# Engine orders, PSUM banks and transfer holds written out as lists, in a gated linear attention followed by a gated feed-forward layer

## The chip, the cores and the metric

The kernel runs on one core of one Trainium2 chip. The metric is the time of one execution in device microseconds (us); lower is better. Five engines work side by side, each with an order of its own: PE (TensorE, the matmuls), ACT (ScalarE), DVE (VectorE), POOL (GpSimd) and SP (SyncE, which here only issues transfers). PE writes only to PSUM, which has eight banks; ACT and DVE read PSUM. DMA engines carry data between HBM and SBUF and, as "DMA transposes", from SBUF to SBUF.

## What is computed

The reference is an attention with a decaying state, then a feed-forward layer (B=4 batches, H=8 heads, S=768 tokens, D=48; model width 384, inner width 1536):

```python
f = 1.0 / (1.0 + np.exp(-f_logit))
for t in range(S):
    state = f[:, :, t, :, None] * state + np.einsum('bhd,bhe->bhde', k[:, :, t], v[:, :, t])
    y[:, :, t] = np.einsum('bhd,bhde->bhe', q[:, :, t], state)
...
gate = np.maximum(x @ w_gate, 0.0)
val = x @ w_val
return (gate * val @ w_out).astype(np.float32)
```

x is y with the heads side by side: 3072 tokens of width 384.

## The kernel before

The sequence is cut into six steps (c = 0 to 5) of 128 tokens. In a step each of the four batches (b) goes through the same attention. ACT turns f_logit into minus the log of the gate (Exp at L631, Ln at L633). PE sums it over the tokens of the step with a triangular matrix ("cum", L640) and over the whole step with a column of ones (L643). ACT takes two exponentials of the sums (L650, L652). POOL multiplies k and q with them; the results are the "hats" (L662, L665). The hats have to be turned so that the head dimension lies on partitions (tile `qkT`): for steps 1 and 2 with PE transposes and a DVE copy (L676, L681), for steps 3 to 5 with a DMA transpose issued by SP (L684). PE forms the scores (L706), DVE masks them into `ptm` (L711), POOL casts v to bf16 (`vpad`, L697). PE adds the part that comes from the old state and the part of the step itself: for steps 0 to 2 in a form that comes out already turned (L733) and that ACT copies to `xT` (L750), for steps 3 to 5 in the natural form (L739, L743), which ACT copies to `xn` (L756) and SP turns by DMA. PE forms k^T v (L767), and DVE and POOL update the state (L480, L482).

Step 0 has a form of its own (`attention_four`, L485, and `attention_back`, L605). Its f, k and q are loaded by `load_four` (L375) with four consecutive tokens of one head in each run of 768 bytes, so that four tokens lie on a partition; all four batches are worked on together, with four cumulative sums for every output (L515, L520), transposes at L555, scores at L574 and masks at L581. `attention_back` turns the k hats back (L613, L618). All other loads (`load`, L393) carry two batches of a step with runs of 192 bytes, 384 KB in each.

The feed-forward part of a step works on all 512 tokens of the four batches. For each of the 12 blocks j of 128 inner units PE forms gate and value (L796, three matmuls each), ACT takes the ReLU of the gate (L802), DVE multiplies (L806) into `gT`. In steps 0 and 1 the first blocks are done for batches 0, 1 and 2, 3 apart, so that the layer can begin when two batches are ready. Then, for each batch, 12 matmuls of 384 columns with `wo` (L819) form the output; ACT copies it (L829), SP stores it.

The weights are read by POOL's transfers, which convert to bf16 (`load_w`, L408): three slices each of `wg`, `wv` and `wo`, four blocks j in each.

The order of the work is set by a list scheduler (`Plan.schedule`, L90): every operation has an engine, an estimated duration and a priority, and the scheduler places one after another at the earliest moment that it estimates, giving PSUM banks from limits by group ("f": 4, "s": 4 and so on, L294). `follows` keeps loads in the order of the step; `flight = 3` makes a load wait until the third load ahead of it has landed (L845); `floor` and "@" in `first` (L233) hold back the first loads. Ahead of the first operations PE multiplies zeros 512 columns wide (L869 to L892), as many as fit in the gaps of the estimate. The engines run their lists in order; between engines there are semaphores (`needs`, L171).

Of the kernel before, what the change touches and what calls it, by code (L numbers as in the profile page):

```python
# [9 lines left out]


class Op:


    __slots__ = ("eng", "emit", "reads", "writes", "occ", "lat", "prio", "opens", "deps",
                 "idx", "start", "end", "pos", "inc", "sem", "val", "snap", "n_left", "users", "ready",
                 "after", "follows", "flow", "goal", "floor")

    def __init__(self, eng, emit, reads, writes, occ, lat, prio, opens=(), after=(), follows=()):
        self.eng, self.emit, self.reads, self.writes = eng, emit, reads, writes  # L20
        self.occ, self.lat, self.prio, self.opens = occ, lat, prio, list(opens)
        self.after, self.follows = list(after), list(follows)
        self.users = []
        self.inc = False
        self.sem = None
        self.val = 0
        self.start = None
        self.flow = None
        self.floor = 0.0


class Bank:


    def __init__(self, group):
        self.group = group
        self.ap = None
        self.ops = []
        self.slot = None


class Plan:


    ENGINES = ("PE", "ACT", "DVE", "POOL", "SP")

    def __init__(self, limits):
        self.ops = []
        self.limits = limits
        self.free0 = {e: 0.0 for e in self.ENGINES}  # L50

    def add(self, eng, emit, reads=(), writes=(), occ=0.5, lat=0.2, prio=0, opens=(), after=(), follows=()):
        op = Op(eng, emit, list(reads), list(writes), occ, lat, prio, opens, after, follows)
        op.idx = len(self.ops)
        self.ops.append(op)
        return op

    def link(self):
        writers, readers = {}, {}
        for op in self.ops:  # L60
            deps = {}
            for d in op.after:
                deps[d] = "raw"
            for d in op.follows:
                deps[d] = "order"
# [4 lines left out]
            for t in op.writes:  # L70
                for r in readers.get(t, ()):
                    if r is not op and deps.get(r, "order") == "order":
                        deps[r] = "war"
                for w in writers.get(t, ()):
                    if w is not op and deps.get(w, "order") == "order":
                        deps[w] = "war"
# [3 lines left out]
            for t in op.writes:  # L80
                if t in op.reads or isinstance(t, Bank):
                    writers.setdefault(t, []).append(op)
                else:
                    writers[t] = [op]
                    readers[t] = []
# [4 lines left out]
    def schedule(self, banks):  # L90
        self.link()
        for op in self.ops:
            op.n_left = len(op.deps)
            op.ready = op.floor
            for d in op.deps:
                d.users.append(op)
        free = dict(self.free0)
        waiting = {e: [] for e in self.ENGINES}
        order = {e: [] for e in self.ENGINES}
        for op in self.ops:  # L100
            if op.n_left == 0:
                waiting[op.eng].append(op)
        slots = [{"ap": ap, "tile": None, "at": at} for ap, at in banks]
        used = {}
        left = len(self.ops)
        flow_free = 0.0

        def banks_for(op):
            n, group = len(op.opens), op.opens[0].group
            if used.get(group, 0) + n > self.limits[group]:  # L110
                return None
            idle = [s for s in slots if s["tile"] is None or all(o.start is not None for o in s["tile"].ops)]
            idle.sort(key=lambda s: s["at"])
            return idle[:n] if len(idle) >= n else None

        while left:
            pick = None
            for e in self.ENGINES:
                for op in waiting[e]:
                    at = max(free[e], op.ready)  # L120
                    slot = ()
                    if op.opens:
                        slot = banks_for(op)
                        if slot is None:
                            continue
                        at = max(at, slot[-1]["at"])
                    key = (at, op.prio, op.idx)
                    if pick is None or key < pick[0]:
                        pick = (key, op, slot)
            if pick is None:  # L130
                raise RuntimeError("no op can be scheduled: " + repr(
                    [(e, len(waiting[e])) for e in self.ENGINES]))
            (at, _, _), op, slot = pick
            e = op.eng
            waiting[e].remove(op)
            for tile, s in zip(op.opens, slot):
                if s["tile"] is not None:
                    for o in s["tile"].ops:
                        op.deps[o] = "war"
# [831 lines left out]
```

## Time and profile before

| what | value |
|---|---|
| median of 3 runs (lowest, highest) | 210.68 us (207.79, 211.08) |
| span of the profiled execution | 208.5 us (a time of its own is not listed beside it) |
| mean granted TensorE clock | 0.967 |
| busy: PE, ACT, DVE, POOL | 191.4, 110.5, 105.1, 79.6 us |
| first matmul of the feed-forward layer | 29.28 us |
| end of the last matmul | 205.66 us |
| bytes read from and written to HBM | 25.95 MB, 4.72 MB |

The span is the time from the first to the last instruction. Busy is the sum of the durations on an engine; a matmul's duration holds its way through the array, so that a row of matmuls on PE counts as busy also where they follow one another less closely than they could. A line of a group reads: line of the code, engine, operation, output and inputs by the program's names, shape, count, busy time, mean duration in ns. "idle before" is the time in which the engine waited ahead of such instructions, and what ended the wait. The chain of waits starts at the last instruction and goes back, at each step, to what released it. In a table by stretches of time, the columns are the time from and to, its length, each engine's busy time with the count of instructions, the granted clock of TensorE, the share of time in which the 16 DMA engines were occupied (over 1 where transfers overlap on them), and GB/s.

### The profile page before, as it was taken

What the parts mean: (1) busy time and instruction counts of PE and PEld (TensorE: products, weight loads), DVE (VectorE), ACT (ScalarE), POOL (GpSimd) and SP (SyncE); (2) the same over time, 40 slices, a digit from 0 to 9 for tenths busy, and PEclk for the clock granted to TensorE, in tenths of its full rate; (3) what the DMA queues carried; (4) which work ended last, traced back from release to release, by engine and by line L of the source; (5) the groups of instructions that cost most, each with busy time, mean ns of one, the idle gap of its engine ahead of it and who ended that gap; (6) DMA issues with size and microseconds to landing.
All of it is one profiled execution on the core that took longest, in us unless ns stands there. A gap on an engine that the chain in (4) does not pass through costs nothing.

```text
span 208.5 us, 4328 instructions
## 1 busy us (share of the span) xinstructions
PE 191.4 (92%) x1724; PEld 110.0 (53%) x1743; DVE 105.1 (50%) x183; ACT 110.5 (53%) x239; POOL 79.6 (38%) x112
## 2 busy tenths in 40 slices
PE   7835779999999799999999999997999999999994
PEld 2414449645677576455555555553545554445562
DVE  7008376643818878657376444634545333323210
ACT  2741224583488678876747756555434334443411
POOL 8806910027196875967553654413500000000000
PEclk9995758999999999999999999999999999999999
DMA  4997899999599999999889999988961111111112
GB/s 130 263 209 152 118 199 190 188 232 211 120 223 237 227 187 197 168 207 204 172 192 138 196 222 160 218 161 145 206 154 36 46 38 41 38 38 38 38 51 103
DMA packets 115076, 31.74 MB, mean 152 GB/s; under 512 B 105072, under 2 KB 115056, under 8 KB 115056
## 3 DMA queue, kind: packets, MB, share of 16 engines
q1 hardware_dynamic: 111072, 27.93, 65.7%
q0 software_dynamic: 3984, 3.54, 10.9%
q8 instruction: 14, 0.23, 0.4%
q14 instruction: 6, 0.05, 0.1%
HBM read 25.95 MB, written 4.72 MB: 147 GB/s over the span
## 4 chain that ended last, share of the span: by engine, by line
PE 84%; DMA 5%; SPq 3%; DVE 2%; ACT 2%; issue 2%; DVEq 0%
PE ps L796 45%; PE ps L819 22%; DMA q_in<-in_q_dram 4%; SPq L385 3%; PE ps L706 3%; PE ps L733 2%; PE ps L767 2%; PE ps L676 2%; PE ps L640 2%; DMA qkT<-hats 1%; PE ps L555 1%; PE ps L880 1%; PE ps L743 1%; PE ps L739 1%; PE ps L574 1%
## 5 line engine op out<-in xcount | busy, mean ns | idle before, releaser
L806 DVE TENSOR_TENSOR gT<-relu,ps 128x512 bf16<-128x512 bf16 (+1 forms) x82 | 50.6, 621 | 58.6 <-PE ps L796 44.5
L802 ACT ACTIVATE relu<-ps 128x512 bf16<-128x512 f32 (+1 forms) x82 | 44.5, 545 | 32.2 <-PE ps L796 29.7
L796 PE MATMUL ps<-xT,wv 128*128 128x512 bf16 (+1 forms) x243 | 60.1, 355 | 0.3 <-issue 0.2
L796 PE MATMUL ps<-xT,wg 128*128 128x512 bf16 (+1 forms) x231 | 57.5, 355 | 1.4 <-ACT xT L750 0.6
L819 PE MATMUL ps<-wo,gT 128*128 128x384 bf16 x288 | 52.1, 326 | 0.0
L819 PEld LDWEIGHTS ps<-wo,gT 128*128 128x128 bf16 x288 | 27.0, 98 | 19.1
L662 POOL TENSOR_TENSOR hats<-k_in,expo 128x384 bf16<-128x384 f32 x20 | 19.9, 1000 | 37.0 <-ACT expo L650 36.8
L796 PEld LDWEIGHTS ps<-xT,wg 128*128 128x128 bf16 x246 | 23.1, 99 | 20.0 <-ACT xT L750 0.9
L796 PEld LDWEIGHTS ps<-xT,wv 128*128 128x128 bf16 x246 | 22.9, 98 | 19.9
L711 DVE TENSOR_TENSOR ptm<-ps,tri 128x512 bf16<-128x512 f32 x40 | 26.0, 685 | 9.3 <-PE ps L706 9.3
L829 ACT ACTIVATE osb<-ps 128x384 f32<-128x384 f32 x24 | 11.7, 489 | 30.5 <-PE ps L819 30.5
L665 POOL TENSOR_TENSOR hats<-q_in,expo 128x384 bf16<-128x384 f32 x20 | 19.8, 1000 | 9.1 <-DMA q_in<-in_q_dram 9.1
L482 POOL TENSOR_TENSOR st<-ssum,dec 128x384 bf16<-128x384 f32 x16 | 13.3, 831 | 16.6 <-DVE ssum L480 16.6
L697 POOL CAST vpad<-v_in 128x384 bf16<-128x384 f32 x24 | 11.7, 507 | 2.4 <-DMA v_in<-in_v_dram 2.3
L650 ACT ACTIVATE expo<-ps 128x384 f32<-128x384 f32 x20 | 9.8, 491 | 2.4 <-PE ps L643 2.2
L480 DVE TENSOR_TENSOR ssum<-ps,st 128x384 f32<-128x384 f32 x16 | 8.9, 553 | 4.3 <-PE ps L767 4.2
L652 ACT ACTIVATE expo<-ps 128x384 f32<-128x384 f32 x20 | 9.9, 495 | 0.0
L631 ACT ACTIVATE f_in<-f_in 128x768 f32<-128x768 f32 x10 | 8.4, 840 | 2.6 <-DMA f_in<-in_f_logit_dram 2.6
L706 PE MATMUL ps<-qkT 48*128 48x128 bf16 x160 | 7.9, 219 | 1.8 <-DMA qkT<-hats 1.5
L750 ACT ACTIVATE xT<-ps 128x384 bf16<-128x384 f32 x12 | 5.8, 492 | 6.9 <-PE ps L733 6.9
L880 PE MATMUL ps<-zeros 128*128 128x512 bf16 x24 | 9.3, 538 | 0.1
L756 ACT ACTIVATE xn<-ps 128x384 bf16<-128x384 f32 x12 | 5.9, 488 | 5.2 <-PE ps L743 5.2
(81 smaller groups left out, 158.2 us busy)
## 6 DMA issues: line engine op xcount, KB each, us to landing
v_in<-in_v_dram SPq DMA_DIRECT2D x12, 384.0 KB, 5.5
out_dram<-osb SPq DMA_DIRECT2D x24, 192.0 KB, 2.2
f_in<-in_f_logit_dram SPq DMA_DIRECT2D x10, 384.0 KB, 4.9
k_in<-in_k_dram SPq DMA_DIRECT2D x10, 384.0 KB, 5.6
q_in<-in_q_dram SPq DMA_DIRECT2D x10, 384.0 KB, 5.6
wg<-in_moe_w_gate_dram POOLq DMA_DIRECT2D x3, 384.0 KB, 7.4
wv<-in_moe_w_val_dram POOLq DMA_DIRECT2D x3, 384.0 KB, 8.5
wo<-in_moe_w_out_dram POOLq DMA_DIRECT2D x3, 384.0 KB, 12.3
```

Of the source, the lines that this page charges most:

```text
L482: add("POOL", lambda: gp.tensor_tensor(t4(s_new), t4(tmp), rate, ALU.mult), [key] + dk, [f"S{b}_{c % 2}"], prio=P + 8, **pool_t(HD))
L662: add("POOL", lambda: gp.tensor_tensor(hk, kin[:, b % 2, :, :], ex[:, 1, :].rearrange("p (h d) -> p h d", h=H), ALU.mult), in_keys("k", c, ...
L665: add("POOL", lambda: gp.tensor_tensor(hq, qin[:, b % 2, :, :], ex[:, 0, :].rearrange("p (h d) -> p h d", h=H), ALU.mult), in_keys("q", c, ...
L697: add("POOL", lambda: gp.tensor_copy(vout, vin.rearrange("p (n j) d -> p n j d", j=2)), in_keys("v", c, b, b + 1) + [f"vpad{vi}"], [f"v_{v ...
L706: mm = te.matmul(s.ap[:, p * C:(p + 1) * C], tokens(c, b, 1, p, lo, lo + D), tokens(c, b, 0, p, lo, lo + D))
L711: add("DVE", lambda j=j, s=s: ve.tensor_tensor(ptm[mi][:, j, :, :], s.ap[:, :].rearrange("p (n t) -> p n t", n=NP), mask, ALU.mult), [s, " ...
L796: mm = te.matmul(bank.ap[:, 0:n], wt[:, kt, j * 128:(j + 1) * 128], xT[xi][:, kt, n0:n1], start=(kt == 0), stop=(kt == NK - 1))
L802: add("ACT", lambda: sc.activation(relu[ri][:, 0:n], gate.ap[:, 0:n], AF.Relu), [gate], [f"relu{ri}"], prio=P, **act_t(n))
L806: add("DVE", lambda: ve.tensor_tensor(gT[gi][:, j, n0:n1], relu[ri][:, 0:n], val.ap[:, 0:n], ALU.mult), [val, f"relu{ri}"], [f"gT{gi}_{j}_ ...
L819: mm = te.matmul(o[b].ap[:, 0:DM], gT[gi][:, j, b * C:(b + 1) * C], wo[:, j, :], start=(j == 0), stop=(j == NJ - 1))
L829: add("ACT", lambda b=b, oi=oi: sc.activation(osb[oi][:, :], o[b].ap[:, 0:DM], AF.Copy), [o[b]], [f"osb{oi}"], prio=P, **act_t(DM))
L880: return te.matmul(spare[:, 0:WARM], zeros[:, 0:128], zeros[:, 0:WARM], start=True, stop=True, skip_group_check=True)
```

## The change

- The scheduler is gone. `ORDER` lists the operations of each engine by number, `BANKS` the PSUM bank of every tile in PE's order, and an operation's engine is now given by the list that it is in. Operations that were ACT's or POOL's alone may stand on another engine: of the ReLUs, 23 are on DVE; of the 48 hats, 20 on DVE and 28 on POOL; of the 16 scalings of the state after step 0, 9 on DVE; of the 24 casts of v, 7 on POOL, 8 on ACT and 9 on DVE; of the 25 output copies, 9 on DVE.
- `HELD` adds waits between transfers: operation 34 (v of step 0, batches 2 and 3), for instance, waits until 35 (a slice of `wg`) has landed. The rule with `flight` is gone.
- Step 0 takes the same path as the others: `load_four`, `attention_four` and `attention_back` are removed, and its f, k, q and v are loaded by two batches with runs of 192 bytes. SP issues 54 loads before (12 of 192 KB, 42 of 384 KB), 48 of 384 KB after.
- `PE_HATS` and `X_WAY`: PE turns the hats of steps 0 and 1 (before: 0, 1 and 2), in two halves; step 0's output comes out turned, step 1's is turned by PE transposes of `xn`, and steps 2 to 5 use DMA transposes (before: 3 to 5). DMA transposes go from 24 to 32.
- The scores of two batches follow each other without other work between them.
- The weights come in slices of 2, 2, 4 and 4 blocks. A slice's columns are shared out among its blocks with a step of 2 or 4, so that `wo` has runs of 2 or 4 rows; `wg` and `wv` are now read by PE with that step when it loads the weights.
- Only step 0 is cut by two batches (for the first four blocks j).
- The very last output block is cut into 256 and 128 columns, with a copy and a store of its own for each.
- The zeros ahead are 256 columns wide and 109 in number, at seven fixed places of PE's list (54, 15, 12, 6, 4, 14 and 4 of them), after a first one of 128 columns.

```diff
+PE_HATS = set(range(0, 8))
+X_WAY = "t" * 4 + "p" * 4 + "x" * 16
+WO = [(0, 2), (2, 2), (4, 4), (8, 4)]
+FIRST = ("f0.0 k0.0 q0.0 v0.0 f0.2 wg0+2 wv0+2 k0.2 q0.2 v0.2 wg2+2 wv2+2 wg4+4 wv4+4 f1.0 k1.0 q1.0 v1.0 wg8+4 wv8+4 "
+         "wo0+2 wo2+2 f1.2 k1.2 q1.2 v1.2 wo4+4 wo8+4").split()
+GROUPS = {0: [(0, 2, 0, 4), (2, 4, 0, 4), (0, 4, 4, 12)]}
+ORDER = {
+    "PE": [
+        24, ~54256, 73, 55, ~15256, 81, 63, ~12256, 61, ~6256, 66, 79, ~4256, 93, 111, 84, ~14256, 117, 109, 99, 71, 69, 89,
...
+    "SP": [
+        27, 25, 32, 26, 29, 34, 28, 33, 39, 40, 41, 42, 47, 49, 50, 48, 367, 373, 368, 661, 369, 515, 371, 197, 370, 202,
...
+HELD = {
+    30: 28, 34: 35, 36: 26, 37: 33, 38: 39, 40: 31, 42: 36, 43: 40, 44: 41, 45: 47, 46: 41, 47: 52, 48: 43, 49: 30,
...
-    def schedule(self, banks):
...
+    def lay_out(self, order, banks, places):
...
+    def w_cols(j):
+        s, n = group[j]
+        return slice(s * 128 + (j - s), (s + n) * 128, n)
...
-            src = bass.AP(tensor=w_out.tensor, offset=s * WJ * 128 * DM,
-                          ap=[[DM, 128], [128 * DM, WJ], [1, DM]])
+            src = bass.AP(tensor=w_out.tensor, offset=j0 * 128 * DM, ap=[[n * DM, 128], [1, n * DM]])
...
-    def load_four(n, c):
...
-    def attention_four(c):
...
+        def scaled(src, xh, xe):
...
+            return {**by("POOL", lambda: gp.tensor_tensor(o, i_, e_, ALU.mult), pool_(HD)),
+                    **by("DVE", lambda: ve.tensor_tensor(o, i_, e_, ALU.mult), dve_(HD))}
...
+        add(f"r{c}{b0}.{j}", {**by("ACT", lambda: sc.activation(rdst, gate.ap[:, 0:n], AF.Relu), act_(n)),
+                              **by("DVE", lambda: ve.tensor_scalar_max(rdst, gate.ap[:, 0:n], 0.0), dve_(n))}, [gate], [f"relu{ri}"], key=P)
...
+        last = g == NC - 1 and b == B - 1
+        cuts = [(0, 256), (256, DM)] if last else [(0, DM)]
...
+    for i, d in HELD.items():
+        pl.ops[i].deps[pl.ops[d]] = "raw"
...
+            if i < 0:
+                for _ in range(~i // 1000):
+                    te.matmul(banks[7][:, 0:~i % 1000], zeros[:, 0:128], zeros[:, 0:~i % 1000], start=True, stop=True, skip_group_check=True)
```

In `ORDER` of SP, 27 is q, 25 f and 26 k of step 0 for batches 0 and 1, 32 k, 29 f and 33 q for batches 2 and 3, 34 and 28 the two v; 39 to 42 are step 1's first f, k, q and v.

More of the change, by code (lines that the diff above doesn't have):

```diff
@@ L9 @@
 BF16 = mybir.dt.bfloat16
[L12 to L29 removed]
+NL = {"f": 4, "k": 5, "q": 5, "v": 5}
@@ L470, in new_state, with hk_, hq_ @@
+        return dma(op, item, "POOL", *flow)
+    for item in FIRST:
+        done[item] = load_w(item) if item[0] == "w" else load(item)
+    def hk_(i):
+        return f"hk{i}"
+    def hq_(i):
+        return f"hq{i}"
     def new_state(kv, c, b, w, P):
```

898 lines of the change are left out of this document (301 added, 597 removed), and 51 rows, old and new, of tables (BANKS, HELD, ORDER).

## The prediction

> **What bounds the kernel now.** I read the page first (busy shares, slices, the chain by engine), then the chain in order of time, then the stretches.
>
> ```profile
> span 208.5 us, 4328 instructions
> ...
> PE 191.4 (92%) x1724; PEld 110.0 (53%) x1743; DVE 105.1 (50%) x183; ACT 110.5 (53%) x239; POOL 79.6 (38%) x112
> ...
> PEclk9995758999999999999999999999999999999999
> ...
> PE 84%; DMA 5%; SPq 3%; DVE 2%; ACT 2%; issue 2%; DVEq 0%
> ```
> ```profile
> 8.17 7.36 DMA q_in<-in_q_dram
> ...
> 28.30 0.93 ACT xT L750 x2
> 29.28 2.10 PE ps L796 x9
> ...
> 142.56 3.11 DMA qkT<-hats
> ...
> 197.85 7.81 PE ps L819 x48
> ```
> ```profile
> 39.20 0.81 PE L796 MATMUL ps<-xT,wv 128*128 128x512 bf16 x3
> ...
> 39.85 0.81 PE L796 MATMUL ps<-xT,wg 128*128 128x512 bf16 x3
> ```
>
> The chain is PE for 84%, and not from the start: until 29.28 us it is loads (step 0's q), hats and masks; then it is the feed-forward matmuls, to 205.66; the last copy and store take 2.8 us more. So three things can shorten it: an earlier start than 29.28, less work or fewer gaps on PE behind it, a shorter tail.
>
> Is PE full between 29.28 and 205.66 (176.4 us)? Its busy time can't say, since durations overlap; start to start can. Three matmuls of 512 columns take 0.65 us (39.20 to 39.85), so 0.216 each; in the chain twelve of 384 take 1.95, so 0.163; by columns 256 take 0.109, 128 take 0.056, 96 some 0.043, 48 some 0.028. Work before: 372 x 0.216 + 120 x 0.109 + 288 x 0.163 = 140.3, and attention about 26 (cum 5.0, transposes 3.6 + 0.9, scores 20 groups of 0.25, outputs 8 x 0.39 + 12 x 0.39, k^T v 3.4, rest). That is 166, so some 10 us of the 176 are gaps, nearly 2 of them the half clock up to 33 us (0.68 granted in 30 to 35, below).
>
> ```profile
> core 0: us, PE busy (x) PEld busy (x) DVE busy (x) ACT busy (x) POOL busy (x), PEclk, DMA share, GB/s
> 25.00:30.00 5.00, 2.88 (x52) 2.12 (x53) 3.68 (x6) 1.47 (x3) 1.82 (x3) 0.64 1.23 201
> 30.00:35.00 5.00, 5.00 (x73) 4.03 (x72) 2.48 (x7) 2.05 (x5) 0.00 (x0) 0.68 1.26 189
> ...
> 45.00:50.00 5.00, 4.95 (x26) 2.33 (x25) 2.36 (x5) 3.92 (x12) 4.23 (x5) 1.00 1.14 215
> ...
> 65.00:70.00 5.00, 4.23 (x95) 3.09 (x97) 3.86 (x9) 3.48 (x12) 3.93 (x5) 1.00 1.19 237
> ...
> 140.00:145.00 5.00, 4.21 (x29) 1.98 (x27) 2.66 (x4) 2.78 (x7) 1.95 (x2) 1.00 0.87 120
> ```
>
> **The front.** Before, q of step 0 is the last of 12 loads and everything waits for it (hats at 15.6), then one pass for four batches. After, the last piece ahead of the first feed-forward matmul in PE's list is the scores of batches 2 and 3, which need q of these: the eighth load of SP. A load of 384 KB (393,216 bytes) takes 1.66 us at 237 GB/s (65 to 70) and 1.83 at 215 (45 to 50); eight take 13.3 to 14.6. First bytes at about 2.3 (issue at 0.81, and the first five us move only 121 GB/s). Four weight slices of two blocks share the engines; they are 0.79 MB of bf16, 3.9 us at 201 GB/s, of which part is beside the loads (share 1.23 with both kinds): I take 2.5, bounds 0 and 3.9. Plus 0.65 to be seen: 19.4. Then the q hats (1.00 on POOL), a transpose group and its copy (0.6 + 0.6), two score groups and gaps (0.8): first feed-forward matmul at 22.5, bounds 20 and 26. That is 6.8 earlier. The old four-token form had the cheaper load (2.36 MB at 272 GB/s is 8.7, now 10 to 11): a cost inside that sum. Zeros: 54 of 256 columns are 5.9 us at full clock, 11.5 at half; PE starts them at 1.26, and the first logs can be ready at about 8.6 (f lands near 6.9, two passes of 0.84), so they cost 0 to 2 us of a chain that q's landing covers. They should keep some clock; I still take 1.5 us lost to half clock behind the start, bounds 0 and 4 (before: 2).
>
> **The holds.** On SP, v of batches 2 and 3 waits for the first `wg` slice, and behind it stand the other v, that q and all of step 1. POOL issues this slice behind five fills (0.2 to 0.9 each by the rows of L321), so near 3.2, and the first slices took 7.4 to 8.5 us to land at twice the size; landing at 7 to 9 it is ahead of the moment when the five loads in front are through (2.3 + 5 x 1.75 = 11): cost 0, bounds 0 and 3, the latter if the slice only lands at 12 and the queue runs dry for a trip. On POOL a later slice waits for v of batches 0, 1 (near 17), and the q hats of batch 2 stand behind it; they need q at 19.4 anyway: 0. From `wg` blocks 4 to 11 on, each slice waits for a load, and the hats of step 1 stand behind on POOL: this is the fifth rival.
>
> **PE's work behind it.** Feed-forward: 408 x 0.216 + 48 x 0.109 + 276 x 0.163 + 1.3 + 0.7 = 140.3, as before. Attention: cum 5.0, transposes of step 1 alone 1.8, scores 5.0, natural outputs 20 x 0.39 = 7.8, turning step 1's xn 0.7, k^T v 2.7, two outputs of step 0 0.5: 23.5. Together 163.8; before 166.
>
> **Gaps.** Before 8 without the clock, 3.1 of them at 142.56, where a DMA transpose of hats came late. Lists cannot be priced from a trace that has none. Bounds: 0 (the stretch 155 to 206 has none) and 13 (8 and 5 more for a busier DVE). I take 5, nearer to before's than to the best: the lists name the engine with room, but they fix an order that real landings must meet. **Tail.** 128 columns: copy 0.28 for 0.49 by the slope of the ReLU rows (597 and 385 ns at 512 and 256), a third of the store: 2.5 for 2.8.
>
> **Off the path.** DVE takes over work: 68 x 0.687 + 48 x 0.685 + 20 x 0.69 + 11 x 0.415 + 20 x 0.545 + 29 x 0.554 + 31 x 0.55 + small = 146 us against 105; about 120 of it lie between 22.5 and the last mask (35 us before PE's end), in some 128 us. Covered, but by little. POOL falls from 80 to some 50. ACT stays near 107. The weight step: PE now reads `wg` and `wv` with a step of 2 or 4. The old k transposes (L613) read their weights with step 4.
>
> ```profile
> L555 PEld LDWEIGHTS ps<-ident,hats 128*128 128x128 bf16 x32 | 2.5, 122 | 6.5 <-DVE hats L543 6.3 <-issue 0.2
> ...
> L613 PEld LDWEIGHTS ps<-ident,qkT 128*128 128x128 bf16 x16 | 1.4, 132 | 0.2 <-issue 0.2
> ```
>
> Step 1 took 122 ns and step 4 132 in the same clock-starved stretch; 98 + 10 lies under a matmul of 216: cost 0, bounds 0 and, for the 48 pieces at 109, nothing visible.
>
> **Sum.** 22.5 + 163.8 + 1.5 + 5 + 2.5 = 195.3 us of span, 13 under 208.5. The runs shown lie from 0.7 below the span to 2.6 above it, the median 2.2 above; I add 1: 196.
>
> **A page against this change.** Rows first:
>
> ```profile
> L538 POOL TENSOR_TENSOR hats<-q_in,expo x2: 991/1148/1304, 15.6 to 16.6; 128x384 bf16<-128x384 f32 x2
> L538 DVE TENSOR_TENSOR hats<-q_in,expo x2: 545/972/1399, 15.6 to 17.9; 128x384 bf16<-128x384 f32 x2
> ```
>
> The product q x exponential reads two SBUF tensors; alone it takes 545 ns on DVE and 991 on POOL, begun together at 15.6 it took 1399 and 1304. Masks and products with a PSUM operand keep to 680 to 694 whatever POOL does. The Trainium skill, "SBUF — State Buffer", Who interferes with whom, says that a DVE instruction with two SBUF inputs and a GpSimd instruction that reads SBUF share a port, and that the later one blocks until the first is done; the trace agrees (1399 is 854 more than 545). By that rule the sum would be that of the first rival.
>
> **Rivals.**
> 1. DVE and POOL block each other. 29 products with two SBUF operands move to DVE. Up to 0.85 each for those that meet POOL (busy some 40 of 128 us): 29 x 0.31 x 0.85 = 8, if all meet, 25. 120 + 8 leaves DVE no room in 128, so most of the 8 turns into PE gaps: 204. For it: 1399; against: the lists may keep them apart.
> 2. SP's queue becomes the bound. Added on it: 8 DMA transposes, four of hats (262 KB) and four of xn (98 KB), at 120 GB/s (140 to 145 moves little else) 12 us; step 0's small runs 1.5 to 2. Before, transfers ended near 155. If none of that queue's idle time is found back, the last hats land at 155 + 12 = 167, less what an end of the flight rule gives; behind the last scores PE's list still has 35 us (81 x 0.216, 64 x 0.163, 4 more, an output group, gaps), then the tail: 204.5, with 1 added 206. For it: share about 1 up to 150 us. Against: with 128 us of queue work (48 x 1.75, 16 x 2 less overlap, stores) there is room before 152.
> 3. Everything fits: gaps 0 to 1, half clock 0, start at 21: 189.
> 4. Slower: the stepped weights. If loading weights with step 2 or 4 took longer than the matmul it hides under, 408 pieces would run at that duration; it decides from 216 ns, and at 270 the time is 196 + 22 = 218. For it only that all 456 hidden matmuls change; against it 132 beside 122. The Trainium skill, "TensorE: Matmul & The Clock Gate", Weight-path perf modes, lets fast weight load take a column step up to 1,024: by that rule, nothing.
> 5. The earlier start is given back: weights for blocks 4 to 11 come later than PE asks (they share with step 1's loads): 6 us lost, 202.
>
> **Numbers.** Forecast 190 to 201 around 196: 0.57. Rival 1: 0.12; 2: 0.12; 3: 0.08; 4: 0.04; 5: 0.07. Two per cent, about what a measurement of this kernel tells from no change, is 206.5 to 214.9. Rival 2 is half faster, a third within; so faster 0.90, same 0.04, slower 0.06 (rival 4 and the tail of 2). Range 188 to 206.
>
> **What would show it.** First feed-forward matmul (L595) at 20 to 26; matmuls of 512 columns still 0.65 for three; PE gaps in the middle 2 to 8 us with the granted clock at 1.0; DVE busy near 146, its two-operand hats (L450) at 545 ns or near 1400; the last load before 150 and the last hats transposed before 152; last store 2.5 us behind the last matmul. Wrong if PE waits for DMA in 30 to 60 us or for DVE throughout, or if LDWEIGHTS of wg leave 98 ns.

## The result and the profile after

The changed kernel takes 219.44 us (median of 4 runs, 218.79 to 220.31); the kernel before took 210.58 beside it. The ratio is 1.048, with a 95% interval of 1.040 to 1.056: slower, where 196 us was forecast. The profiled execution took 218.81 us with a span of 217.1.

From the page of the changed kernel, to be set beside that of before:

```profile
span 217.1 us, 4047 instructions
...
PE 193.1 (89%) x1604; PEld 115.3 (53%) x1622; DVE 135.7 (62%) x243; ACT 97.4 (45%) x215; POOL 51.6 (24%) x72
...
PEclk9999999669999997999999799999999999999999
...
PE 47%; DMA 21%; SPq 14%; DVE 7%; issue 5%; POOL 4%; ACT 2%; POOLq 0%; DVEq 0%
```

The front is what was forecast: the clock row of the page has no dip ahead of slice 8 (before, the fourth to sixth digits were 5, 7 and 5), and the first feed-forward matmul starts at 23.35 us, 5.9 earlier. What is new is in the last line. PE's share of the chain fell from 84 to 47%, and DMA with SP's issues (SPq) rose from 8 to 35%. The three dips in the clock, at slices 8 and 9, 16 and 23, say where. The stretches around them:

```profile
core 0: us, PE busy (x) PEld busy (x) DVE busy (x) ACT busy (x) POOL busy (x), PEclk, DMA share, GB/s
35.00:40.00 5.00, 1.65 (x15) 0.85 (x15) 2.67 (x5) 0.60 (x1) 4.14 (x6) 1.00 1.03 193
40.00:45.00 5.00, 4.00 (x27) 2.03 (x27) 3.04 (x6) 1.93 (x3) 2.34 (x3) 0.50 1.22 211
80.00:85.00 5.00, 1.87 (x30) 1.07 (x28) 2.46 (x5) 2.07 (x3) 0.53 (x2) 0.93 0.87 159
85.00:90.00 5.00, 4.78 (x24) 2.41 (x23) 3.00 (x6) 2.55 (x9) 2.91 (x3) 0.72 1.19 163
115.00:120.00 5.00, 2.26 (x12) 1.00 (x10) 3.33 (x6) 1.50 (x3) 0.51 (x1) 1.00 1.03 195
120.00:125.00 5.00, 4.10 (x27) 2.04 (x29) 3.17 (x5) 2.01 (x3) 0.00 (x0) 0.69 0.92 183
```

In 35 to 40, 80 to 85 and 115 to 120 us PE is idle for 3.35, 3.13 and 2.74 us, and each time the granted clock drops behind it. A full row for PE has 5.00 and clock 1.00. So I make one measure for all runs: over the 25 stretches of 5 us from 25 to 150, idle is the sum of (5 - PE busy), and the half-clock loss is the sum of 5 x (1 - clock). Before: 5.6 and 3.4 us. After: 18.75 and 6.85.

The chain in order of time (start, length, what) names what PE waited for at these places:

```profile
20.29 15.28 DMA q_in<-in_q_dram
...
37.77 3.20 POOL hats L449 x3
...
80.11 3.24 DMA qkT<-hats
...
83.59 0.62 PE ps L493 x16
...
102.31 5.36 DMA k_in<-in_k_dram
...
115.95 4.49 DMA qkT<-hats
...
120.68 0.62 PE ps L493 x16
```

Around 37 us it is step 1's first q and v: q is 15.28 us on its way (the median is 5.6); v, issued at 23.14, lands after 13.9, at 37.04. POOL casts it at 37.17, and the k^T v (L575) that PE's list has next starts at 37.92. At 83.35 and 120.43 hats land from a DMA transpose, and the scores (L493) that PE's list has next start 0.24 us later. At 102.31 step 3's k for batches 2 and 3 is only issued; SP's list sends two v and a k of step 5 ahead of it (at 82.70, 95.94 and 101.81). All of these came over SP's queue. Added up from SP's rows, it is occupied for 144.3 of the first 150 us, and no pause is longer than 0.8; before it was occupied for 118.4, with pauses of up to 12.7. Its rows up to the moment when PE goes on:

```profile
76.95 4.40 SPq L469 DMA_TRANSPOSE qkT<-hats  x2
81.40 1.26 SPq L556 DMA_TRANSPOSE xT<-xn  x1
82.70 0.58 SPq L352 DMA_DIRECT2D v_in<-in_v_dram  x1
83.33 1.96 SPq L556 DMA_TRANSPOSE xT<-xn  x1
```

Transposes and loads stand in one line; the two issues of hats alone hold it for 4.40 us. (SP isn't counted in the page's busy times; a row's length is how long the issue held it.)

The third stall shows the line best. The last of its hats is computed on DVE at 108.92, and by the program its transpose waits for hats alone; yet SP comes to it at 115.95, seven us later, behind two transposes and three loads of steps 4 and 5:

```profile
107.70 1.22 DVE L450 TENSOR_TENSOR hats<-k_in,expo 128x384 bf16<-128x384 f32 x2 [0.20 <-DMA k_in<-in_k_dram]
...
109.17 1.20 SPq L556 DMA_TRANSPOSE xT<-xn  x1
110.42 0.58 SPq L352 DMA_DIRECT2D k_in<-in_k_dram  x1
111.04 1.29 SPq L352 DMA_DIRECT2D v_in<-in_v_dram  x1
112.38 2.85 SPq L469 DMA_TRANSPOSE qkT<-hats  x1
115.27 0.58 SPq L352 DMA_DIRECT2D q_in<-in_q_dram  x1
115.95 2.60 SPq L469 DMA_TRANSPOSE qkT<-hats  x1
```

The profile's chain goes through DVE's rows in this stretch (108.37 to 115.95), but this transpose doesn't need them.

The queue's work was finished early, though: the last load lands at 134.1 us (before 150.2), the last hats at 150.6 (before 156.5). But PE had 64 us of work left at 150.6; before, it had some 55 at the same moment. 150.6 + 64 + the tail of 2.4 is the span. The pieces named came later than PE's list wanted them, not the last piece later than before.

### The profile page after: what moved, and what is told of

It reads as the page before. It is cut to its first block, busy times and chain, and to the rows that moved or that the text cites. A ratio compares the mean times of both kernels' runs of the same rounds, so it can differ in the third digit from the quotient of the medians.

```text
span 217.1 us, 4047 instructions
## 1 busy us (share of the span) xinstructions
PE 193.1 (89%) x1604; PEld 115.3 (53%) x1622; DVE 135.7 (62%) x243; ACT 97.4 (45%) x215; POOL 51.6 (24%) x72
## 4 chain that ended last, share of the span: by engine, by line
PE 47%; DMA 21%; SPq 14%; DVE 7%; issue 5%; POOL 4%; ACT 2%; POOLq 0%; DVEq 0%
PE ps L595 26%; PE ps L616 14%; SPq L352 13%; DMA q_in<-in_q_dram 7%; DMA f_in<-in_f_logit_dram 5%; DMA k_in<-in_k_dram 5%; DMA qkT<-hats 4%; POOL hats L449 2%; PE ps L493 2%; DVE gT L603 2%; DVE hats L450 1%; PE ps L539 1%; PE ps L426 1%; DVE ptm L501 1%; DVE relu L601 1%
## 5 line engine op out<-in xcount | busy, mean ns | idle before, releaser
L595 PE MATMUL ps<-xT,wv 128*128 128x512 bf16 (+1 forms) x219 | 53.9, 372 | 2.6 <-issue 1.6
L616 PE MATMUL ps<-wo,gT 128*128 128x384 bf16 (+2 forms) x300 | 53.8, 322 | 0.0
L600 ACT ACTIVATE relu<-ps 128x512 bf16<-128x512 f32 (+1 forms) x53 | 30.1, 577 | 40.9 <-PE ps L595 31.0
L501 DVE TENSOR_TENSOR ptm<-ps,tri 128x512 bf16<-128x512 f32 x48 | 30.3, 682 | 10.5 <-PE ps L493 10.5
L449 POOL TENSOR_TENSOR hats<-k_in,expo 128x384 bf16<-128x384 f32 x13 | 13.2, 1022 | 29.4 <-DMA k_in<-in_k_dram 14.1
L601 DVE TENSOR_SCALAR relu<-ps 128x512 bf16<-128x512 f32 (+1 forms) x23 | 14.9, 651 | 5.3 <-PE ps L595 5.2
L622 ACT ACTIVATE osb<-ps 128x384 f32<-128x384 f32 (+2 forms) x16 | 7.5, 470 | 21.0 <-PE ps L616 15.8
L450 DVE TENSOR_TENSOR hats<-q_in,expo 128x384 bf16<-128x384 f32 x9 | 6.1, 683 | 15.4 <-ACT expo L437 15.4
L668 PE MATMUL ps<-zeros 128*128 128x256 bf16 x109 | 15.3, 301 | 0.0
L493 PE MATMUL ps<-qkT 48*128 48x128 bf16 x192 | 8.2, 224 | 7.4 <-DMA qkT<-hats 6.5
L437 ACT ACTIVATE expo<-ps 128x384 f32<-128x384 f32 x24 | 11.5, 492 | 2.6 <-PE ps L429 1.9
L668 PEld LDWEIGHTS ps<-zeros 128*128 128x128 bf16 x109 | 11.5, 108 | 2.2
L493 PEld LDWEIGHTS ps<-qkT 48*128 48x128 bf16 x192 | 5.9, 97 | 12.2 <-issue 5.3
L575 PE MATMUL ps<-vpad,hats 128*128 128x96 bf16 x80 | 6.7, 210 | 4.8 <-POOL vpad L479 2.8
```

What stands on the lines that cost most here:

```text
L437: add(f"eq{c}{b}", by("ACT", lambda: sc.activation(ex[:, 0, :], bc.ap[:, 0:HD], AF.Exp, scale=-1.0), act_(HD)), [bc], [f"expq{ei}"], key=P ...
L449: return {**by("POOL", lambda: gp.tensor_tensor(o, i_, e_, ALU.mult), pool_(HD)), **by("DVE", lambda: ve.tensor_tensor(o, i_, e_, ALU.mult ...
L493: x = te.matmul(s[b, j].ap[:, p * C:(p + 1) * C], qkT[lo:lo + D, qi, 1, p, :], qkT[lo:lo + D, qi, 0, p, :])
L501: add(f"m{c}{b}{j}", by("DVE", lambda b=b, j=j, mi=mi: ve.tensor_tensor(ptm[mi][:, j, :, :], s[b, j].ap[:, :].rearrange("p (n t) -> p n t" ...
L595: z = te.matmul(bank.ap[:, 0:n], wt[:, kt, w_cols(j)], xT[xi][:, kt, n0:n1], start=(kt == 0), stop=(kt == NK - 1))
L600: add(f"r{c}{b0}.{j}", {**by("ACT", lambda: sc.activation(rdst, gate.ap[:, 0:n], AF.Relu), act_(n)), **by("DVE", lambda: ve.tensor_scalar_ ...
```

## The experiments

My theory after the result: transfers land later than the lists were made for, because all go over SP's queue and PE waits in a fixed order. Rivals: the new holds; the stepped weights; DVE and its port; a bad order on SP alone. Ratios below are to the kernel before, measured beside each run.

### The holds, all of them and those off SP

```diff
-    for i, d in HELD.items():
+    for i, d in {}.items():
```


> All 35 holds between transfers taken out, the lists kept. Theory A (transfers: the DMA engines' time, 169 us of it in the first 150, and one in-order queue on SP pace the middle of the kernel): the same bytes go through the same queue, so 216 to 222 us, and PE's stalls between 80 and 140 us stay (4.1 us in 100 to 105). Theory B (the holds themselves, above all that of a wo slice on POOL, behind which v and the hats of step 1 stand, cost it): 200 to 207 us, and the stall of 3.2 us at 34.7 goes. Theory C (PE's fixed order asks for the next step's attention too early): 214 to 220 us, only the stall at 34.7 goes.

```diff
-        pl.ops[i].deps[pl.ops[d]] = "raw"
+        if i in ORDER["SP"]:
+            pl.ops[i].deps[pl.ops[d]] = "raw"
```


> Only the holds on POOL's weight slices taken out, those on SP's loads kept. Theory B with POOL as the place: 205 to 213 us, the stall of 3.2 us at 34.7 goes. Theory A: 216 to 222 us. Theory C: 214 to 220 us.

Measured: 220.54 us (1.046, 1.037 to 1.055) and 220.72 (1.046, 1.035 to 1.058), the same as with all holds. The holds aren't the cause. They even help at the first stall: without them PE stands for 6.15 us ahead of 42.25 (6.32 ahead of 41.91 with SP's alone), for 2.78 ahead of 37.92 with them. POOL then issues the next weights at 28.9 to 30.3 at once, and v of step 1 is only there at 41.4.

### Long runs in all loads

```diff
-        src = bass.AP(tensor=srcs[n].tensor, offset=b0 * H * S * D + c * C * D, ap=[[D, C], [S * D, (b1 - b0) * H], [1, D]])
-        dst = ld[n][:, slot_of(n, c, b0 // 2), b0 % 2:b0 % 2 + b1 - b0, :, :].rearrange("p b h d -> p (b h) d")
+        src = bass.AP(tensor=srcs[n].tensor, offset=(2 * c + b0 // 2) * 2 * C * HD, ap=[[2 * HD, C], [1, 2 * HD]])
+        dst = ld[n][:, slot_of(n, c, b0 // 2), :, :, :].rearrange("p b h d -> p (b h d)")
```


> Every load of q, k, v and f takes as many bytes, but in one run of 3072 bytes for each partition in place of 16 runs of 192 (it reads other tokens than the reference asks for). Theory A: packets of 192 bytes took 16.7 ns, of 768 bytes 42.7 in the kernel before, so the loads' share of the engines' time falls from 103 us to some 50 to 60, and the time to 193 to 204 us, with the stalls between 80 and 140 nearly gone. Theory B: 213 to 219 us. Theory C (a wrong order, whatever the landings): 212 to 219 us.

Measured: 198.46 us (0.941, 0.930 to 0.953). Every list, bank and hold is the changed kernel's; only the loads have the same bytes in longer runs (128 of 3,072 bytes in each). From the page of this run:

```profile
span 197.9 us, 4065 instructions
...
PEclk9999999978999999999999999999999999999999
...
PE 72%; DVE 9%; DMA 9%; ACT 5%; issue 2%; POOL 1%; SPq 1%; DVEq 0%
```

and two of the stretches that had the stalls:

```profile
80.00:85.00 5.00, 4.61 (x57) 3.00 (x56) 4.39 (x8) 2.07 (x4) 1.84 (x3) 1.00 0.96 225
...
115.00:120.00 5.00, 5.00 (x34) 2.88 (x32) 5.00 (x12) 3.94 (x10) 1.48 (x3) 1.00 1.02 197
```

Idle is 4.7 us instead of 18.75, half-clock loss 1.7 instead of 6.85: 19.2 us of the 21.0 by which the two medians differ. The mean issue of a load holds SP for 0.53 us, where it was 1.82, so SP is occupied for 73 of the first 150 us and not 144; and its transfers occupy the 16 DMA engines for 105 us, where it was 148.5 (share of SP's queue times the span). So this is shown: with loads that are there in time, these lists run as I forecast. DVE's work and the stepped weights are the same in this run, so neither makes the loss by itself. What isn't told apart is whether the long issues or the occupied engines made the loads late.

### Small transposes

```diff
-    ... sy.dma_start(qkT[:, qi, :, :, :].rearrange("p x n t -> p (x n) t"), hats[:, hi, :, :, :].rearrange("p x h d -> p (x h d)"), transpose=True)
+    ... sy.dma_start(qkT[:, qi, 0, 0, :], hats[:, hi, 0, 0:2, :].rearrange("p h d -> p (h d)"), transpose=True)
-    ... sy.dma_start(xdst, xn[ni][:, :], transpose=True)
+    ... sy.dma_start(xdst[:, 0, :], xn[ni][:, 0:C], transpose=True)
```


> The DMA transposes are cut: those of hats turn one block of eight, those of xn one of three, the rest of their output is left as it was (the product is not the reference's). Issues, waits and loads are as before. Theory A in the form that the transposes stand behind prefetched loads in SP's queue and cost 30 us of engine time: 203 to 212 us. Theory A in the form that the loads' bytes alone pace it: 213 to 218 us. Theory B and C: 214 to 220 us.

Measured: 216.7 us (1.027, 1.018 to 1.037). The time on the engines falls as much as it should, from 148.5 to 118.6 us, and only 2.7 us of the time follow. The shortest issue of a transpose is 1.09 us with one block and 1.24 with eight: the bytes go and the issue stays. SP's rows in this run at two times, and the engines' share (second number from the end) at both:

```profile
79.02 3.39 SPq L469 DMA_TRANSPOSE qkT<-hats  x2
82.45 1.23 SPq L556 DMA_TRANSPOSE xT<-xn  x1
83.73 0.58 SPq L352 DMA_DIRECT2D v_in<-in_v_dram  x1
84.35 2.58 SPq L556 DMA_TRANSPOSE xT<-xn  x1
...
102.19 1.97 SPq L352 DMA_DIRECT2D k_in<-in_k_dram  x2
104.20 1.74 SPq L352 DMA_DIRECT2D v_in<-in_v_dram  x1
105.99 1.67 SPq L352 DMA_DIRECT2D q_in<-in_q_dram  x1
107.70 1.77 SPq L625 DMA_DIRECT2D out_dram<-osb  x1
...
80.00:85.00 5.00, 4.31 (x43) 2.42 (x42) 4.31 (x7) 3.19 (x6) 0.95 (x2) 1.00 0.48 99
102.00:109.00 7.00, 5.87 (x43) 2.88 (x38) 3.10 (x6) 4.93 (x14) 1.99 (x2) 1.00 1.08 231
```

Each row starts some 0.04 us behind the one before. Where SP issues transposes, it is full while the engines' share is 0.48; where it issues loads, the engines are full too (1.08), and a load holds SP about as long as its transfer takes (384 KB at 231 GB/s are 1.70 us). SP is occupied for 143.8 of the first 150 us, as in the changed kernel, and a mean load still takes 1.87 us to issue. So occupied engines alone aren't the bound, and behind loads they may well be what holds SP.

### The order on SP alone, and all lists made anew

```diff
     "SP": [
-        27, 25, 32, 26, 29, 34, 28, 33, 39, 40, 41, 42, 47, 49, 50, 48, 367, 373, 368, 661, 369, 515, 371, 197, 370, 202,
+        25, 29, 27, 34, 33, 26, 32, 28, 42, 40, 50, 39, 369, 49, 515, 41, 47, 367, 48, 520, 370, 368, 514, 371, 517, 197, 373,
...
```


> The holds are out, as in the run without holds (220.5 us), and one list is changed besides: SP's. Its 105 transfers are the same, put in another order, which was found with a model that takes 2.25 us for a load in place of the 1.56 that the kernel's own price of 0.0122 us a packet gives; the lists of PE, ACT, DVE and POOL are as they were. Theory A1 (only the amount of transfer time counts): 217 to 222 us. Theory C, now as: SP's list sends pieces of steps 4 and 5 (v of step 5 at 82.7 and 95.9 us, k of step 5 at 101.8) ahead of those that PE's list asks for next (k of step 3 at 102.3, k of step 4 at 122): 209 to 214 us.

Here the order on SP comes from a small model of mine fed with measured durations, without holds. Measured: 220.22 us (1.043, 1.034 to 1.053). Between 55 and 145 us PE's idle time is about half of what it was (7.9 us for 14.2), but the front is lost: the first feed-forward matmul comes at 27.08, and PE stands 7.34 us ahead of 48.90 since step 1's q lands at 47.6. Idle in all is 18.3.

```diff
     "SP": [
         27, 25, 32, 26, 29, 34, 28, 33, 39, 40, 41, 42, 47, 49, 50, 48,
-        367, 373, 368, 661, 369, 515, 371, 197, 370, 202,
+        372, 370, 367, 368, 374, 371, 369, 519, 373, 514, 383,
...
```


> SP's list is changed from its 17th transfer on (steps 2 to 5, stores and turns); steps 0 and 1 and their holds stay as they are, since the run with the whole of SP's list changed lost in the front (first feed-forward matmul at 28.6 us, a stall of 7.8 us at 41) what it won behind it (7.6 us of stalls between 54 and 145 us for some 18). All other lists are as they were. Theory C (order of SP's list): 210 to 215 us. Theory A1 (only the amount): 217 to 221 us.

The front is kept with its holds; the order is new from the 17th on, without holds. Measured: 220.76 us (1.039, 1.029 to 1.048). Idle is 19.2: new waits on DVE's and ACT's lists, which weren't changed to suit (PE waits 1.32 us for an exponential ahead of 135.16, 2.33 for a mask ahead of 139.52 and 0.94 for an output copy ahead of 141.29, while feed-forward blocks of step 3 are ready but stand further down in its list).

```diff
     "SP": [
-        27, 25, 32, 26, 29, 34, 28, 33, 39, 40, 41, 42, 47, 49, 50, 48, 367, 373, 368, 661, 369, 515, 371, 197, 370, 202,
+        27, 25, 32, 26, 29, 34, 28, 33, 39, 40, 41, 42, 47, 49, 50, 48, 367, 369, 368, 371, 513, 370, 373, 391, 374, 383, 659,
...
```


> All five lists and the banks are changed behind the front, for a load of 2.2 us in place of 1.56; the instructions are the same ones (some products and copies change their engine), the transfers are the same, steps 0 and 1 load as they did. Theory C in the wide form (the lists fit transfers that are faster than the chip's): 203 to 210 us. Theory A1 (the amount of transfer alone, whatever the order): 216 to 221 us.

The lists of all five engines and the banks come from the model here, with the holds of the front alone. Measured: 218.4 us (1.031, 1.023 to 1.039). One stall of 7.43 us ahead of 38.69: on ACT a ReLU stands behind the cast of step 1's v, which was issued at 24.26 and landed at 37.82. So the order on SP can't be mended alone, and my model was no better a base for lists than the one that they came from. That other lists would suit the true landings is neither shown nor refuted.

### Long runs in part, and in the kernel before

```diff
+        if c == 0:     (first run; second run: if n in "kq":)
+            src, dst = the two lines with long runs, as above
```


> Only the eight loads of step 0 are in runs of 3072 bytes in place of 192 (they read other tokens). Theory A1: they take some 8 us less of the engines' time, step 1's loads come by as much earlier, and the time is 210 to 214 us. If the time of the middle is set by the order alone (C): 216 to 220 us, since only the front starts earlier.

> Half of the loads, those of k and q, in runs of 3072 bytes (other tokens are read); lists and holds as they were. If the time follows the transfer time one to one, half of the 21 us that all loads together gave: 207 to 211 us. If a threshold decides (the lists hold once a load is near 1.56 us on average, as their price says): 199 to 204 us.

Measured: step 0 alone 217.53 us (1.036, 1.030 to 1.041), k and q of all steps 205.2 (0.968, 0.962 to 0.975). Half of the loads give 14.2 of the 21.0 us, and no half clock is left (0.0; idle 11.7). Step 0's gives 1.9; the later loads carry the loss.

```diff
     def load(n, c, b0, b1, after=()):
...
+        src, dst = the two lines with long runs, as above      (in the kernel before)
```


> The kernel before with the loads of steps 1 to 5 in runs of 3072 bytes (other tokens are read; step 0 keeps its runs of 768 bytes). If the kernel before too is paced by transfers: 199 to 205 us. If its list, made with dearer transfers and at most three loads in flight, hides them already: 207 to 212 us, its PE gaps of 8 us being those of the front and of one late transpose.

Measured: 208.89 us (0.992, 0.988 to 0.995, 10 runs). The same edit (here of steps 1 to 5; step 0 has runs of 768 bytes already) gives 1.8 us in the kernel before and 21.0 in the changed one. SP is occupied here for 60 of the first 150 us and not 118, its transfers for 97 us of engine time and not 137, and PE has little use for it: idle and half clock were 9.0 together and become 6.5. So before was nearly free of these waits, and the changed kernel isn't.

### The weights in plain slices

```diff
-        return slice(s * 128 + (j - s), (s + n) * 128, n)
+        return slice(j * 128, (j + 1) * 128)
...
-            src = bass.AP(tensor=w_out.tensor, offset=j0 * 128 * DM, ap=[[n * DM, 128], [1, n * DM]])
+            src = bass.AP(tensor=w_out.tensor, offset=j0 * 128 * DM, ap=[[DM, 128], [128 * DM, n], [1, DM]])
```


> The weights are taken in blocks of 128 neighbouring columns again, and w_out's rows in blocks to match. If reading weights with a step of 2 or 4 costs PE anything that shows (rival 4): 212 us or less. If it lies under the matmuls, as LDWEIGHTS of 110 ns beside 98 under matmuls of 216 says: 218 to 222 us.

Measured: 222.11 us (1.057, 1.051 to 1.062): not faster. Its weight loads take 101 and 99 ns (wg, wv), with the step 110 and 109; both hide under a matmul of 216. The rival falls.

### Fewer issues, the same bytes

```diff
-        else:
-            op = add(f"xh{c}{b}", ... qkT[:, qi, :, :, :] ... hats[:, hi, :, :, :] ... transpose=True
+        elif b % 2:
+            op = add(f"xh{c}{b}", ... qkT[:, qi - 1:qi + 1, :, :, :] ... hats[:, hi - 1:hi + 1, :, :, :] ... transpose=True
```


> The DMA transposes of the hats of two batches are one transfer each (8 issues in place of 16, standing where the later one stood; the same bytes; all other lists and holds as they were). Theory A2: SP issues without a pause from 0.8 to 150 us, and what paces it is the issue of a DMA transpose, 1.25 us each however small, in which the engines run dry; 8 fewer give up to 10 us: 209 to 215 us. Theory A1 (bytes and packets): 217 to 221 us, or more, since the earlier batch now waits for the later.

> As e12, and the DMA transposes of xn too are taken by pairs (8 in place of 16; xT is laid out by batches for it, PE reads it with four pieces of 128 columns). Theory A2: another 10 us less of SP's time, 203 to 212 us. Theory A1: 216 to 221 us.

The second one turns the outputs by pairs too (`xT` as `[128, B, NK, C]`). Measured: 218.45 us (1.038, 1.032 to 1.043) and 216.55 (1.026, 1.017 to 1.035): 1.0 and 2.9 us better, the first not clear of noise. A pair of hats takes 1.86 us at least to issue, two singles 2.5, so pairs save little there; a pair of outputs takes 1.2, which is half.

### Step 2's turns: put into the kernel before, taken out of the changed one

```diff
-    pe_hats = {1, 2}
-    x_way = {0: "tiled", 1: "tiled", 2: "tiled", 3: "xbar", 4: "xbar", 5: "xbar"}
+    pe_hats = {1}
+    x_way = {0: "tiled", 1: "tiled", 2: "xbar", 3: "xbar", 4: "xbar", 5: "xbar"}
```


> The kernel before with step 2's hats and outputs turned by DMA as well, as the changed kernel does it (8 more DMA transposes; its scheduler makes a new list). Theory A2: 10 us more of SP's issue time, in a kernel whose loads end 56 us ahead of its end: 214 to 221 us. Theory A1: 262 and 98 KB more are 2 to 3 us of the engines' time, 209 to 213 us.

Measured: 219.34 us (1.044, 1.036 to 1.052): eight DMA transposes more, with the list that its scheduler makes for them, cost the kernel before 9.2 us (210.13 beside it), as much as the whole change. Two of its stretches:

```profile
90.00:95.00 5.00, 2.04 (x32) 1.45 (x32) 2.26 (x5) 2.87 (x7) 4.21 (x6) 0.72 0.91 187
95.00:100.00 5.00, 3.81 (x18) 1.77 (x20) 0.35 (x1) 2.92 (x10) 3.03 (x4) 0.50 0.91 176
```

Idle goes from 5.6 to 10.1, half clock from 3.4 to 10.2: in these ten us PE stands for 4.15 and loses 3.9 more to the clock. In its chain a load of f lands at 93.11, a turned output of step 2 (3.64 us as DMA) at 96.76, and the feed-forward matmuls that read it start at 97.20. SP isn't full here (115.8 of the first 150 us). PE's rows in these ten us have five waits: for masks (1.17 and 0.65 us), for a cast of v (1.40), for the log of that f (1.02), and only the last, 0.98, for the turned output. So the run shows what eight more transposes cost, and not that one late transpose does it.

```diff
-PE_HATS = set(range(0, 8))
-X_WAY = "t" * 4 + "p" * 4 + "x" * 16
+PE_HATS = set(range(0, 12))
+X_WAY = "t" * 4 + "p" * 4 + "t" * 4 + "x" * 12
```


> The changed kernel with step 2's hats turned on PE and its outputs written turned, as the kernel before does both: 8 DMA transposes fewer (24 for 32), 8 transpose groups and 8 copies more (some 4 us of PE work, copies on DVE and ACT); everything else of the five lists in its place. Theory A2, as the kernel before with eight more turns shows it (219.3 us for 210.1): 209 to 213 us. Theory A1: 217 to 221 us.

> As e15, and the 24 remaining DMA transposes are taken by pairs, 12 issues. Theory A2: 4 to 8 us less than e15, 203 to 209 us. Theory A1: 217 to 221 us.

The second one has the pairs for steps 3 to 5 as well. Measured: 214.57 us (1.025, 1.015 to 1.035) and 211.77 (1.011, 1.002 to 1.020), that is 4.9 and 7.7 us better, although PE has more to do. SP is occupied for 129 of the first 150 us in both, idle is 12.8 and 10.0. In the chain of the first, DMA's share falls from 21 to 9%, SP's issues keep theirs (14 and 15%). So the eight added transposes are a part of the loss, 4.9 of the 8.9 us to before net of PE's added work, and nothing that I tried on these lists, with all transfers in their true size, got below the kernel before.

### The transposes on ACT's queue

```diff
-    op = add(f"xh{c}{b}", by("SP", lambda: sy.dma_start(...transpose=True), ...
+    op = add(f"xh{c}{b}", by("ACT", lambda: sc.dma_start(...transpose=True), ...     (outputs likewise; numbers moved to ACT's list)
```


> The changed kernel with all 32 DMA transposes issued by ACT in place of SP (the same transfers, placed in ACT's list where their input was ready; holds, loads, stores and the other lists as they were). ACT's busy part of 97 us gets 32 issues of about 1.25 us more. Theory A2 (while SP issues a transpose, the engines run out of loads: none moved from 80.5 to 83.5 us): loads flow beside the transposes, SP's queue ends 10 to 20 us earlier, 206 to 214 us, less what ACT's ReLUs come later. Theory A1 (packets and bytes alone): 218 to 224 us.

> As the run with step 2 on PE and the rest by pairs (211.8 us), with its 12 DMA transposes issued by ACT. Theory A2: 203 to 209 us, below the kernel before. Theory A1: 211 to 215 us.

The second one is the same for step 2 on PE with pairs (e16). Measured: 227.88 us (1.077, 1.072 to 1.083) and 213.91 (1.013, 1.010 to 1.017): 8.4 worse, and no gain over the pairs on SP. I had taken the DMA engines to run dry behind SP's transposes. That reading was wrong. In the changed kernel, per microsecond:

```profile
80.00:81.00 1.00, 0.47 (x3) 0.00 (x0) 0.90 (x2) 0.01 (x1) 0.53 (x2) 1.00 1.27 178
81.00:82.00 1.00, 0.00 (x0) 0.00 (x0) 0.82 (x2) 0.97 (x2) 0.00 (x0) 1.00 0.96 190
82.00:83.00 1.00, 0.00 (x0) 0.00 (x0) 0.00 (x0) 0.70 (x1) 0.00 (x0) 1.00 1.00 199
83.00:84.00 1.00, 0.41 (x15) 0.44 (x16) 0.00 (x0) 0.00 (x0) 0.00 (x0) 1.00 0.15 30
```

Their share is 1.27, 0.96 and 1.00 while PE waits. The load ahead (f, issued at 75.19) lands at 81.0 and the next is issued at 82.70, so in between it is all transposes; only in the last row is the share 0.15. With the transposes on ACT, f of step 4 (batches 0 and 1) lands at 91.2 instead of 94.0, but its log ends at 101.0 instead of 96.0: ACT is late, the data isn't. The Trainium skill, "DMA: Bandwidth & Descriptors", Rules for kernel authors, says that spreading DMAs over several issuing engines adds no bandwidth and only saves the sequencer's issue time. These two runs agree in that neither gains, and here the saved issue time was paid for on ACT.

## Why the prediction was wrong

Measured is a span of 217.1 us, 21.8 more than the sum.

- **First feed-forward matmul**: 23.35 for 22.5. Right, 0.85 off.
- **The step that failed: "Gaps. ... I take 5", with "1.5 us lost to half clock".** Measured 18.75 and 6.85, so 25.6 for 6.5: 19.1 of the 21.8. Even the bounds (13 and 4) were too low. I wrote that lists "fix an order that real landings must meet", and then priced it by before's gaps. With e3's loads the same lists have 4.7 and 1.7, 6.4 in all: the terms hold only if transfers are in time. Before's gaps were misread too: the 3.1 us at 142.56 are how long that transfer was on its way; PE stood 1.30 of them, by its row in the kernel before.

```profile
145.71 0.40 PE L706 MATMUL ps<-qkT 48*128 48x128 bf16 x8 [1.30 <-DMA qkT<-hats]
```

- **Why they weren't: the second rival.** I gave it 0.12 and a test: "there is room before 152". The test was met (last load 134.1, last hats 150.6), and the rival came true in another form. The queue needn't end late: without a pause in it, every piece comes when its turn comes, and a list that wants it earlier stands. I should have compared each landing with its place in PE's list, not the queue's total with its end. The engine time was priced about right (11.5 us more, 137.0 to 148.5, where I had 13.5 to 14 for transposes and small runs). Left out was SP itself: I counted "128 us of queue work", and it was occupied for 144.3 of the first 150 us, 26 more than before. The loads were priced right (87 us for 84); the transposes stood at 32 and held SP for 52 (16 issues of 1.80 us in the mean, 16 of 1.45). My sign for "wrong", a wait for DMA in 30 to 60 us, was met by the first stall. That stall also has the fifth rival's mechanism, loads beside weights, but what came late was step 1's v and not the weights.
- **The holds** at 0: right (e1, e2). **Stepped weights** at 0: right in time; weight loads did leave 98 ns, for 110, so the sign that I named for "wrong" was a bad one: it should have been a duration near 216. **Zeros**: the first 54 end as the first sum starts, at 9.44, some 1.5 us behind the first log; the chain runs through SP's loads there, so this is within the 0 to 2 and off the path. They start 0.21 us apart until about 5.3 and 0.11 later: half speed at first, which the page's clock row doesn't show. **Tail**: 2.4 for 2.5.
- **DVE** is busy 135.7 us for 146. The two-operand hats that I feared:

```profile
L450 DVE TENSOR_TENSOR hats<-q_in,expo 128x384 bf16<-128x384 f32 x9 | 6.1, 683 | 15.4 <-ACT expo L437 15.4
```

683 ns for 545 alone: on 20 such products some 2.8 us. Slow ones met POOL (1,001 ns at 52.43, beside a POOL product from 52.03 to 53.02). The first rival's mechanism shows, its size doesn't.
- **Own time over span**: 1.7 for 1; the median lies 0.6 above that. The remaining 2 of the 21.8 us aren't placed: PE's idle time behind 150 us is 0.5.

The measures of the main runs side by side, in us (SP: occupied in the first 150 us; engines: SP's transfers on the 16 DMA engines, over the span; lost: idle and half clock, 25 to 150):

| run | SP | engines | lost | ratio |
|---|---|---|---|---|
| before | 118.4 | 137.0 | 9.0 | 1 |
| before, long runs (e7) | 60.3 | 96.8 | 6.5 | 0.992 |
| after | 144.3 | 148.5 | 25.6 | 1.048 |
| long runs (e3) | 73.3 | 105.1 | 6.4 | 0.941 |
| long runs for k, q (e11) | 114.7 | 127.4 | 11.7 | 0.968 |
| small transposes (e4) | 143.8 | 118.6 | 21.6 | 1.027 |
| pairs (e13) | 136.1 | 149.7 | 18.7 | 1.026 |
| step 2 on PE (e15) | 129.0 | 134.0 | 16.2 | 1.025 |
| step 2 on PE, pairs (e16) | 129.2 | 137.5 | 15.1 | 1.011 |

In the table's runs with the changed kernel's lists the loss falls with SP's column and not with the engines' alone: e4 has fewer engine microseconds than e15 or e11 and loses more. Step 0's long runs (e6) free SP ahead of 25 us alone, and so lose 24.2 still. The runs without holds have SP at 140.6 and 138.4 and lose 26.3 and 25.5, and e14 (lists of its own) loses 20.3 with 115.8, so the column orders these runs and is no law. The runs with ACT's queue and with new orders stand outside this, since there something else is late. (Each row is of one profiled execution; e13's was its fastest, 214.20 us.)

How far is the cause settled? Shown: most of the loss is PE waiting, at the three places named, for what SP's queue brings (9.3 of the 18.75 us of idle time by PE's rows, and the 6.85 of half clock behind them), and 19.2 of the 25.6 us go away when the loads get longer runs with nothing else changed. Shown: less time on the engines alone gives 2.7 us (e4), fewer issues with the same bytes 2.9 (e13), both for eight transposes 4.9 (e15). Not told apart: what the rest of a load's 1.82 us on SP is. The shortest issue of such a load is 0.44 us. At their shortest (0.44, 1.24 for hats, 1.18 for outputs, 0.33 for a store) all 105 issues would hold SP for some 68 us, an estimate from these rows; so more than half of the 144.3 is SP standing behind something, and whether that is the engines or the queue isn't shown. Open too: which lists would suit the true landings. The lists that I derived (e5, e9, e10) moved the stall instead of removing it.

## What to carry to other kernels

When an order by a scheduler's estimate becomes a fixed list, check each transfer's landing against the place in the list that first needs it; that the queue was done before the end said nothing here. In a kernel whose transfer queue has no idle time, price an added transfer by what it pushes back, both in engine time and in issue time. A stall that halves the clock costs more than its own length: here 1.7 us more behind 3.13 and 3.42, and 3.4 behind the first.

## What the runs showed of the hardware

- **Issue time on SP.** A load of 384 KB holds SP for 1.82 us in the mean with 2,048 runs of 192 bytes and for 0.53 with 128 of 3,072 (e3); the shortest take 0.44 and 0.33. The shortest issue of a DMA transpose is 1.24 us for eight blocks, 1.18 for three, 1.09 for one (e4) and 1.86 for sixteen (e12): up to eight blocks nearly all of it is per issue.
- **Weights starve loads.** In 24 to 26 us of the changed kernel the 192-byte packets moved 13 GB/s while the weights' 1,024-byte packets moved 170; loads by themselves moved 231 (10 to 13 us). The q that was on its way then took 15.28 us.
- **The clock.** By PE's rows it stood for 2.78 us ahead of 37.92 and 0.57 ahead of 39.84, 3.13 ahead of 83.59 and 3.42 ahead of 120.68. Half clock ran from 39.98 to 46.80, from 84.35 to 87.76 and from 121.89 to 125.30 us, that is for 6.82, 3.41 and 3.41. The Trainium skill, "TensorE: Matmul & The Clock Gate", What's actually happening, has the clock halve after one idle window of about 3.4 us that runs freely. The trace agrees in the length, and the three starts lie 13.0 and 11.0 times 3.41 us apart, as on one grid. It differs in the trigger: no stretch of 3.41 us ahead of a start was idle throughout. They held 1.9, 2.7 and 2.2 us without a matmul; two stretches of the same grid with 1.4 (from 33.15 and from 135.55) left the clock full.
